# A transformer block on one core: the two row halves of the PE array get job lists of their own, with 14, 11 or 12 matmul steps a cycle

## The chip, the cores and the metric

The kernel runs on one core of a Trainium2 chip. The metric is the time of one execution on the device in microseconds (us); the median of three runs before the change is 1439.39 us. The engines are named as in the profile: PE (matmul), PEld (its weight loads), DVE (VectorE), ACT (ScalarE), POOL (GpSimd) and SP, which issues most of the transfers (DMAs).

## The reference

One pre-norm transformer block over 2048 tokens of width 512, in float32: 32 query heads of size 16 share one key head and one value head, and a gated feed-forward part of width 1792 follows.

```python
h  = x + attention(layernorm(x))       # q = x @ wq (32 heads of 16), k = x @ wk, v = x @ wv (one head)
                                       # softmax(q k^T / 4) v, heads joined, @ wo
h2 = h + (gelu(n @ w_gate) * (n @ w_up)) @ w_down      # n = layernorm(h), gelu by the tanh formula
```

## The kernel before

**Two programs woven into one.** The tokens are cut into four blocks of 512. The attention of block b runs side by side with the dense part (output projection, second norm, feed-forward) of block b-1; the dense part of the last block runs alone at the end (the tail). PE, SP and DVE work in the order in which the program writes their instructions; all three take them strictly in turn in the part that matters here.

**Attention.** A head group is four heads. For each of its 16 key chunks there are two score steps. A score step (`scores`, L358 and L362) is two matmuls on the two row halves of the array and one exp on ACT over 128x1024 elements; it needs one of two PSUM buffers `s`, so that a third step waits until the first one's exp is done. Later `weigh` (L366) multiplies the exps of a key chunk with the values, into the bank `acc`. So a head group has 32 score steps and 16 weighings.

**Cycles.** `SIZES = (6, 5, 5, 6, 5, 5)` cuts the 32 score steps of a head group into six cycles, which this document numbers 0 to 5. In a cycle the score steps come one after the other, and behind each stand some steps of dense work; all weighings that are ready stand at the cycle's end (2, 3, 2, 3, 3 and 3 key chunks in cycles 0 to 5). With cycle 5 the head group is complete, and `evacuate` sends it on: DVE copies `acc` to `oT` (L379), SP stores it to `acc_d` (L380), waits until that has landed, and issues four loads of it in another layout, `oc` (L390). At the fifth score step of a head group SP issues two loads of the queries of the next one (`load_q`, L343).

**Dense work.** Each product is split in two halves of 64 rows of the contraction, and the array's two row halves work at the same time. A step is one matmul of 64 rows on each half. `duo` (L507 to L529) computes two products at once, in two turns of 12 steps: in the first turn the lower rows work on the first product and the upper rows on the second, in the second turn the other way round. A one-column copy on DVE, `mark` (L527), stands between the turns, since both halves of a product add into the same PSUM bank. Three banks are there for products. Every cycle holds one turn, so 12 steps:

```python
LONG = {5: (0, 5, 4, 3, 0), 6: (0, 5, 3, 3, 1, 0)}    # dense steps behind each score step
```

**Feed-forward.** Per block there are 14 pieces f of the width 1792. `up(f)` computes gate and up products for a piece; the gate's tanh goes to ACT at the end of a later cycle (`gates`), and DVE forms the result, split in a high and a low part. `down` multiplies the results of four pieces (`RUNS`) with `w_down`, as four products of 12 terms for the four 128-token parts. The weights lie in DRAM, already split in high and low parts. `load_w1` (L499) loads both weights of a piece at once, 1 MB, into one of two buffers, two pieces ahead, as soon as the piece that used the buffer is done. `load_w2` (L504) loads 1 MB of `w_down` for two pieces, two loads at a time, into three buffers.

**Order of cycles.** The dense part of a block takes 47 cycles (`kinds`): four of 12 steps for the output projection, one gap, 40 of 12 steps, and two short ones. For the first block it begins with cycle 3 of a head group (`LEAD`), for the second and third with cycle 2.

Of the kernel before, what the change touches and what calls it, by code (L numbers as in the profile page):

```python
# [19 lines left out]
P = 128  # L20
# [4 lines left out]
BOUND_MAX = 30.0  # L25
BOUND_PAD = 1.02
PB = 5

FIRST_Q = 1

# [12 lines left out]
def kernel(  # L43
# [56 lines left out]
    q_d = dram.tile([H, KR, S], F32R, name="q_d")  # L100
    acc_d = dram.tile([P, 4, T], F32, name="acc_d")

    w1_d = dram.tile([FC, P, 2, 2, DC, P], F32R, name="w1_d")
    w2_d = dram.tile([FC, P, 2, D], F32R, name="w2_d")

    def split(eng_hi, hi, lo, src, eng_lo=None):
# [38 lines left out]
    def run(outer, first):  # L145
# [231 lines left out]
        def evacuate(b, g, acc):  # L377
# [17 lines left out]
                nc.vector.reciprocal(oc[:, 1, sl], oc[:, 1, sl])  # L395

            def divide():
                if c == 0:
                    o_blk[b] = [
                        sb.tile([P, DC, T], F32R, tag=f"o_{w}", bufs=1, name=f"o_{w}_{b}")  # L400
                        for w in ("hi", "lo")
                    ]
                hi, lo = o_blk[b]
                nc.vector.tensor_tensor(oc[:, 0, :], oc[:, 0, :], oc[:, 1, :], op=ALU.mult)
                split(nc.vector, hi[:, c, :], lo[:, c, :], oc[:, 0, :])


            def piece(t):
# [12 lines left out]
            if b == NB - 1 and g == NG - 1:  # L421
                last_out.append(piece)
            elif k == 1:

                outs.extend([[] for _ in range(4 if b == 0 else 1)])
                outs.extend([partial(invert, t), partial(invert, t + 1)] for t in (0, 2))
                outs.append([divide])
            if b == 0 and g == NG - 1:
                while outs:
                    take_out()  # L430
# [4 lines left out]
        def part_weights(pw):  # L435
# [24 lines left out]

            def store_1(f, k, both):
                nc.gpsimd.dma_start(
                    w1_d[f, :, :, k].bitcast(F32),
                    both.rearrange("p i (c n) -> p i c n", c=DC).bitcast(F32),
                )

# [27 lines left out]
                yield 1  # L494
            left()

        def load_w1(b, f):
            w = db.tile([P, 2, 2, DC, P], F32R, tag="w1", bufs=2, name=f"w1_{b}_{f}")
            nc.sync.dma_start(w.bitcast(F32), w1_d[f].bitcast(F32))  # L499
            return w[:, 0], w[:, 1]  # L500

        def load_w2(b, j):
# [6 lines left out]
        def duo(names, terms):  # L509

            banks = [psum1(n) for n in names]
            n = len(terms[0])
            for turn in range(2):
                for i in range(n):
                    for a in range(2):
                        k = (turn + a) % 2
                        lhsT, rhs = terms[k][i]
                        rows = slice(64 * a, 64 * a + 64)
                        nc.tensor.matmul(  # L519
                            banks[k], lhsT[rows], rhs[rows], start=(turn == 0 and i == 0),  # L520
                            stop=(turn == 1 and i == n - 1), skip_group_check=True,
                        )
                    yield 1
                if turn == 0:

                    mark = sb.tile([P, 1], F32, tag="mark", bufs=2, name=f"mark_{names[1]}")
# [19 lines left out]
        def dense(b, tail=False):  # L546
# [14 lines left out]
            w1 = {0: load_w1(b, 0), 1: load_w1(b, 1)}  # L561
            if b == 0:
                yield 0
            w2 = {}
# [129 lines left out]

            yield from start_tail() if tail else start()

            def up(f, gh, gl):
                hi, lo = w1.pop(f)
                terms = [
                    [  # L700
                        (wt[:, k, c, :], xt[:, c, :])
                        for c, (wt, xt) in (
                            [(c, (w, xT_hi)) for c in range(DC) for w in (hi, lo)]
                            + [(c, (hi, xT_lo)) for c in range(DC)]
                            if tail
                            else [
                                (c, z)
                                for c in range(DC)
                                for z in ((hi, xT_hi), (hi, xT_lo), (lo, xT_hi))
                            ]  # L710
                        )
                    ]
                    for k in range(2)
                ]
                pg, pu = yield from product([f"pg_{b}_{f}", f"pu_{b}_{f}"], terms)
                g = db.tile([P, T], F32, tag="g", bufs=2, name=f"g_{b}_{f}")
                nc.vector.tensor_copy(g, pg)  # L717
                a = db.tile([P, T], F32, tag="ga", bufs=2, name=f"ga_{b}_{f}")
                nc.vector.tensor_tensor(a, g, g, op=ALU.mult)
                nc.vector.scalar_tensor_tensor(  # L720
                    a, a, 1.0 / GELU_A, g, op0=ALU.add, op1=ALU.mult
                )

                def gate():
                    nc.scalar.activation(a, a, AF.Tanh, scale=GELU_A * GELU_C)  # L725
                    nc.vector.scalar_tensor_tensor(a, a, 1.0, g, op0=ALU.add, op1=ALU.mult)  # L726
                    nc.vector.tensor_tensor(a, a, pu, op=ALU.mult)
                    split(nc.vector, gh[:, f % 2, :], gl[:, f % 2, :], a)

                gates.append(gate)
                if tail:
                    open_gates()
                yield CUT

            def down(fs, gs, last):
                tw = [w2.pop(f // 2) for f in fs[::2]]
                for t0 in range(0, TB, 2):
                    terms = []  # L740
                    for t in (t0, t0 + 1):
                        sl = slice(t * P, (t + 1) * P)
                        terms.append([
                            (gt[:, k, sl], wt[:, k, :])
                            for (gh, gl), (hi, lo) in zip(gs, tw)
                            for k in range(2)
                            for gt, wt in ((gh, hi), (gh, lo), (gl, hi))
                        ])
                    pds = yield from product(
                        [f"pd_{b}_{fs[0]}_{t0}", f"pd_{b}_{fs[0]}_{t0 + 1}"], terms  # L750
                    )
                    for t, pd in zip((t0, t0 + 1), pds):
                        nc.vector.tensor_tensor(hs[t], hs[t], pd, op=ALU.add)
# [4 lines left out]
            prev = None  # L758
            for fs in RUNS:

                early_f = 2 if fs is RUNS[-1] else 1
                gs = []
                for n, f in enumerate(fs):
                    if f % 2 == 0:
                        gs.append([
                            db.tile([P, 2, T], F32R, tag=tag, bufs=3, name=f"{tag}_{b}_{f}")
                            for tag in ("gh", "gl")
                        ])
                    yield from up(f, *gs[-1])
                    if f + 2 < FC:  # L770
                        w1[f + 2] = load_w1(b, f + 2)
                    if fs is RUNS[-1] and n == 0:
                        w2[f // 2] = load_w2(b, f // 2)
                    if n + 1 == early_f and prev is not None:
                        yield from down(*prev, False)
                    if fs is not RUNS[-1] and n + 1 == early_f:
                        for g in fs[::2]:
                            w2[g // 2] = load_w2(b, g // 2)
                prev = (fs, gs)
            yield from down(*prev, True)  # L780

        PER = NG * KC
        work = None
# [9 lines left out]
                    evacuate(pb, pg, pacc)  # L793

        gates, behind = [], []

        def open_gates():
            while gates:
# [93 lines left out]
        for c in range(LEAD[0], (NB - 1) * NG * len(SIZES)):  # L892
# [9 lines left out]
                kind = todo.pop(0)  # L902
            if kind == "long":
                shares = LONG[size]
            elif kind == "short":
# [4 lines left out]
            ready, gates[:] = gates[:], []  # L910
            for j, share in enumerate(shares):
                score(n)
                n += 1

                if b > 0 and cb == 1 and j == 3 and outs:
                    take_out()
# [10 lines left out]
                    elif said == CUT:  # L927
                        break

            while work is not None and kind is not None and said not in (CUT, GAP):  # L930
                said = next(work)
                assert said < 0, said
            for gate in ready:
                gate()
# [6 lines left out]
            if outs:  # L941
                take_out()
        fixed.close()
        assert not outs
        held_banks.close()
# [333 lines left out]
```

## Time and profile before

| | |
|---|---|
| median of three runs | 1439.39 us (1439.32 to 1439.87) |
| the profiled execution | 1439.57 us, its span 1437.9 us |
| busy share of the span | PE 98%, ACT 72%, PEld 52%, DVE 37%, POOL 15% |
| granted clock of the array | 0.999 on average |
| chain that ended last | PE 80%, ACT 14%, DVE 2% |
| bytes moved | 180.54 MB, mean 126 GB/s |
| loads of dense weights on SP | 84 of 1 MB |

Matmuls are pipelined and their ends are modelled, so a busy PE isn't an array at its peak: the starts of the matmuls tell more than their lengths. A line of a timeline gives the start in us, the length, the engine, the line of the kernel, the operation and its operands, how many are merged into the line, and in brackets how long the engine was idle before and what ended that. The line number L519 is that of the matmul in `duo`, L541 that in the tail.

### The profile page before, as it was taken

How to read it: one execution, taken by the hardware profiler on the slowest of the kernel's cores; microseconds unless marked ns; L12 is line 12 of the kernel's file. 1: busy time of each engine (PE TensorE's matmuls, PEld its weight loads, DVE VectorE, ACT ScalarE, POOL GpSimd, SP SyncE). 2: the span in 40 equal slices, each digit the busy share in tenths (PEclk: the TensorE clock that was granted, in tenths of full speed). 3: DMA queues.
4: the chain of work that ended last, by engine and by line, in shares of the span. 5: the costliest groups of instructions: out<-in, count | busy, mean ns of one | idle time of the engine just before them, and what ended most of it. 6: DMA issues, size and time to landing. Idle time of an engine off the chain costs nothing.

```text
span 1437.9 us, 24767 instructions
## 1 busy us (share of the span) xinstructions
PE 1407.6 (98%) x10420; PEld 751.0 (52%) x10420; DVE 537.3 (37%) x931; ACT 1040.1 (72%) x1145; POOL 222.3 (15%) x301
## 2 busy tenths in 40 slices
PE   6999999999999999999999999999999999999998
PEld 5533333225555555555555555554455555557886
DVE  7422322213251423334251423423342432426665
ACT  7699999996777777776777777777777777772000
POOL 5566677731000000000000000000000000000000
PEclk9999999999999999999999999999999999999999
DMA  4456767642223332213332332203333232333551
GB/s 156 150 188 203 216 220 230 204 166 81 108 97 113 115 113 86 86 42 118 129 115 85 115 114 86 85 27 118 131 98 114 88 112 81 129 125 111 197 195 71
DMA packets 58863, 180.54 MB, mean 126 GB/s; under 512 B 8540, under 2 KB 8540, under 8 KB 51544
## 3 DMA queue, kind: packets, MB, share of 16 engines
q1 hardware_dynamic: 48912, 144.79, 29.9%
q0 software_dynamic: 9760, 34.08, 7.3%
q8 instruction: 84, 1.38, 0.4%
q14 instruction: 35, 0.29, 0.1%
q10 hardware_dynamic: 72, 0.00, 0.0%
HBM read 131.13 MB, written 47.71 MB: 124 GB/s over the span
## 4 chain that ended last, share of the span: by engine, by line
PE 80%; ACT 14%; DVE 2%; issue 1%; POOL 0%; DMA 0%; SPq 0%; ACTq 0%; DVEq 0%; POOLq 0%
PE acc L366 31%; PE s L358 18%; ACT p L362 14%; PE pu L519 6%; PE pd L519 6%; PE pg L519 5%; PE pq L184 3%; PE pg L541 3%; PE pd L541 3%; PE pu L541 3%; PE pp L519 2%; PE pxt L594 1%; PE pk L1066 0%; DVE st L1034 0%; PE pqn L222 0%
## 5 line engine op out<-in xcount | busy, mean ns | idle before, releaser
L362 ACT ACTIVATE p<-s 128x1024 f32<-128x1024 f32 x1024 | 970.4, 1057 | 249.7 <-PE s L358 249.1
L366 PE MATMUL acc<-p,v_sb 128*32 128x512 f32 x4096 | 492.3, 598 | 0.2 <-DVE oT L379 0.2
L358 PE MATMUL s<-qg,kaug 50*128 50x512 f32 x1984 | 394.2, 435 | 10.8 <-ACT p L362 7.9
L358 PEld LDWEIGHTS s<-qg,kaug 50*128 50x128 f32 x1984 | 171.5, 184 | 294.8 <-ACT p L362 183.0
L366 PEld LDWEIGHTS acc<-p,v_sb 128*32 128x32 f32 x4096 | 109.8, 109 | 239.2 <-issue 227.0
L519 PE MATMUL pg<-x2h,w 64*128 64x512 f32 x672 | 231.8, 391 | 0.0
L519 PE MATMUL pu<-x2h,w 64*128 64x512 f32 x672 | 231.7, 391 | 0.0
L120 POOL TENSOR_SCALAR rstd<-mv 128x1 f32<-128x1 f32 x16 | 3.5, 219 | 994.5 <-DVE mv L118 994.2
L519 PE MATMUL pg<-x2l,w 64*128 64x512 f32 x336 | 131.3, 391 | 0.0
L519 PE MATMUL pu<-x2l,w 64*128 64x512 f32 x336 | 131.3, 391 | 0.0
L519 PEld LDWEIGHTS pg<-x2h,w 64*128 64x128 f32 x672 | 124.7, 186 | 11.7
L519 PEld LDWEIGHTS pu<-x2h,w 64*128 64x128 f32 x672 | 124.7, 186 | 11.7
L519 PE MATMUL pd<-w,gh 64*128 64x512 f32 x672 | 105.4, 391 | 0.0
L725 ACT ACTIVATE ga<-ga 128x512 f32<-128x512 f32 x56 | 35.8, 639 | 89.1 <-DVE ga L720 89.1
L717 DVE COPY g<-pg 128x512 f32<-128x512 f32 x56 | 38.5, 688 | 118.5 <-PE pg L519 112.9
L726 DVE SCALAR_TENSOR_TENSOR ga<-ga,g 128x512 f32<-128x512 f32 x56 | 38.8, 692 | 88.9 <-ACT ga L725 88.9
L519 PEld LDWEIGHTS pd<-w,gh 64*128 64x128 f32 x672 | 63.2, 185 | 14.9 <-issue 0.7
L519 PE MATMUL pd<-w,gl 64*128 64x512 f32 x336 | 66.4, 391 | 0.0
L519 PEld LDWEIGHTS pu<-x2l,w 64*128 64x128 f32 x336 | 62.3, 185 | 7.4
L519 PEld LDWEIGHTS pg<-x2l,w 64*128 64x128 f32 x336 | 62.3, 185 | 7.3
L527 DVE COPY mark_pu<-pu 128x1 f32<-128x1 f32 x42 | 6.6, 158 | 159.1 <-PE pu L519 159.1
L395 DVE RECIPROCAL oc<-oc 128x128 f32<-128x128 f32 x64 | 56.0, 919 | 24.9 <-DMA oc<-acc_d 23.8
(233 smaller groups left out, 1281.4 us busy)
## 6 DMA issues: line engine op xcount, KB each, us to landing
w<-w_d SPq DMA_DIRECT2D x84, 1024.0 KB
qg<-q_d SPq DMA_DIRECT2D x62, 200.0 KB
q_d<-qh SPq DMA_DIRECT2D x32, 256.0 KB
acc_d<-oT SPq DMA_DIRECT2D x32, 256.0 KB
oc<-acc_d SPq DMA_DIRECT2D x128, 64.0 KB
w_d<-w_0b POOLq DMA_DIRECT2D x14, 512.0 KB, 3.4
w_d<-w_1b POOLq DMA_DIRECT2D x14, 512.0 KB, 3.5
x<-in_A_x_dram SPq DMA_DIRECT2D x16, 256.0 KB
```

The lines of the kernel that those rows point to most:

```text
L184: nc.tensor.matmul(pq, wt[:, d, c * P : (c + 1) * P], xt[:, d, :], start=(n == 0), stop=(n == 3 * DC - 1),)
L358: nc.tensor.matmul(s[:, a, :], kaug[rows, kc * P : (kc + 1) * P], qg[rows, u, :], start=True, stop=True,)
L362: nc.scalar.activation(p[:, 2 * u : 2 * u + 2, :], s, AF.Exp, scale=SCALE)
L366: nc.tensor.matmul(acc[32 * j : 32 * j + 32, :], v_sb[:, kc, :], p[:, j, :], start=(kc == 0), stop=(kc == KC - 1), skip_group_check=True,)
L395: nc.vector.reciprocal(oc[:, 1, sl], oc[:, 1, sl])
L519: nc.tensor.matmul(banks[k], lhsT[rows], rhs[rows], start=(turn == 0 and i == 0), stop=(turn == 1 and i == n - 1), skip_group_check=True,)
L527: nc.vector.tensor_copy(mark, banks[1][:, :1])
L541: nc.tensor.matmul(bank, lhsT, rhs, start=(i == 0), stop=(i == len(ts) - 1))
L594: nc.tensor.transpose(pt[:, c, :], xns[t][:, c * P : (c + 1) * P], ident)
L717: nc.vector.tensor_copy(g, pg)
L725: nc.scalar.activation(a, a, AF.Tanh, scale=GELU_A * GELU_C)
L726: nc.vector.scalar_tensor_tensor(a, a, 1.0, g, op0=ALU.add, op1=ALU.mult)
```

## The change

The 40 cycles of `duo` turns become 36 woven cycles and four as before. All gate, up and down products of a block but those of the last two runs of `down` go into one list, `plan` (28 gate and up products, and eight down products: four behind piece 5, four behind piece 9). `weave` gives each half of the array a job of its own: either the first half of the next product of the list, or the second half of a product whose first half the other half of the array has done. The upper rows start six steps (`LAG`) after the lower ones; six steps are kept as well between the end of a product's first half and the start of its second one, and between the end of a product and the next use of its bank. One half's last matmuls no longer fall together with a cycle's end. The cycles of six score steps now hold 14 steps, the others 11, and the last one of a head group 12.

The weights of a piece are now stored and loaded as two halves, gate and up, of 512 KB each, with four buffers; a buffer's next load, four halves ahead, is issued when its product is done. The loads of `w_down` for the next run are issued when the last down product of a run is done (the first two, when piece 1 is done). The work on DVE is reordered: copies out of PSUM at once, the square and cubic of the gate (`soon`), the steps behind the tanh and those of the head group's division (`lazy`) one at a time, one at each score step; the up product is multiplied in before the tanh, and its bank is free then. A woven cycle puts all its tanhs at its own end. The tail runs as before but for the order of those DVE steps, the halved loads, and the first two `down`s one piece later.

```diff
-        w = db.tile([P, 2, 2, DC, P], F32R, tag="w1", bufs=2, ...)
-        nc.sync.dma_start(w.bitcast(F32), w1_d[f].bitcast(F32))
+        w = db.tile([P, 2, DC, P], F32R, tag="w1", bufs=W1, ...)          # W1 = 4
+        nc.sync.dma_start(w.bitcast(F32), w1_d[i].bitcast(F32))
...
+        def next_w1(i):
+            if i + W1 < 2 * FC:
+                w1[i + W1] = load_w1(b, i + W1)
+        def up_plan(f, k, then):
...
+            def done(bank):
+                (leave_up if k else leave_gate)(f, bank)
+                next_w1(2 * f + k)
+                if k:
+                    then()
...
+        def weave(plan):
...
+            def choose(a):
+                for e in live:
+                    if e["half"] != a and not e["both"] and e["at"] and step >= e["at"] + LAG:
+                        e["both"] = True
+                        return [e, 0]
+                free = opened < width or ends.get(opened - width, step) + LAG <= step
+                if opened == len(plan) or not free or a == 1 and step < LAG:
+                    return None
+                name, terms, done = plan[opened]
...
+            while opened < len(plan) or live:
+                for a in range(2):
+                    if jobs[a] is None:
+                        jobs[a] = choose(a)
+                for a in range(2):
...
+                    nc.tensor.matmul(
+                        e["bank"], lhsT[rows], rhs[rows], start=i == 0 and not e["both"],
+                        stop=last and e["both"], skip_group_check=True,
+                    )
+                step += 1
...
+                    if e["both"]:
+                        e["done"](e["bank"])
+                        ends[e["i"]] = step
+                    else:
+                        nc.vector.tensor_copy(mark, e["bank"][:, :1])
+                        e["at"] = step
+                yield 1
...
-        kinds = ["long"] * 4 + ["gap"] + ["long"] * (2 * FC + 4 * (len(RUNS) - 1)) + ["short"] * 2
+        WOVEN = {6: (0, 5, 3, 3, 3, 0), 5: (0, 5, 3, 3, 0)}
+        LAST = (0, 5, 4, 3, 0)
+        kinds = (
+            ["long"] * 4 + ["gap"] + ["woven"] * 6 * len(SIZES) + ["long"] * 4 + ["short"] * 2
+        )
...
                 score(n)
                 n += 1
+                if soon or lazy:
+                    (soon or lazy).pop(0)()
```

More of the change, by code (lines that the diff above doesn't have):

```diff
@@ L560, in dense @@
             xT_lo = db.tile([P, DC, T], F32R, tag="x2l", bufs=1, name=f"x2l_{b}")
-            w1 = {0: load_w1(b, 0), 1: load_w1(b, 1)}
+            w1 = {i: load_w1(b, i) for i in range(W1)}
             if b == 0:
@@ L695, in dense, with leave_gate @@
             yield from start_tail() if tail else start()
[L697 to L715, printed above, removed]
+            gs, g_of = {}, {}
+            def next_w1(i):
+                if i + W1 < 2 * FC:
+                    w1[i + W1] = load_w1(b, i + W1)
+            def leave_gate(f, pg):
                 g = db.tile([P, T], F32, tag="g", bufs=2, name=f"g_{b}_{f}")
@@ L732, in up @@
-                gates.append(gate)
-                if tail:
-                    open_gates()
-                yield CUT
-            def down(fs, gs, last):
+                    if f % 2 == 0:
+                        gs[f // 2] = [
+                            db.tile([P, 2, T], F32R, tag=tag, bufs=3, name=f"{tag}_{b}_{f}")
+                            for tag in ("gh", "gl")
+                        ]
+                    hi, lo = (z[:, f % 2, :] for z in gs[f // 2])
+                    lazy.append(partial(
+                        nc.vector.scalar_tensor_tensor,
+                        a, a, 1.0, g, op0=ALU.add, op1=ALU.mult,
+                    ))
@@ new lines, in down_plan, with terms, done @@
+            def down_plan(fs, t, tw, then):
+                def terms():
+                    if t == 0:
+                        assert not gates and not lazy or all(j // 2 in gs for j in fs)
+                        open_gates()
+                        while lazy:
+                            lazy.pop(0)()
+                        tw.extend(w2.pop(f // 2) for f in fs[::2])
+                    return down_terms(fs, tw, t)
+                def done(bank):
+                    add_down(t, bank)
+                    if t == TB - 1:
+                        then()
+                return f"pd_{b}_{fs[0]}_{t}", terms, done
@@ L738, in down @@
+            def down(fs, last):
                 tw = [w2.pop(f // 2) for f in fs[::2]]
                 for t0 in range(0, TB, 2):
[L740 to L748, printed above, removed]
+                    terms = [down_terms(fs, tw, t) for t in (t0, t0 + 1)]
@@ L756, in down, with fetch_w2 @@
                     yield CUT
-            prev = None
+            def fetch_w2(fs):
+                for f in fs[::2]:
+                    w2[f // 2] = load_w2(b, f // 2)
+            plan, prev = [], None
             for fs in RUNS:
-                early_f = 2 if fs is RUNS[-1] else 1
-                gs = []
                 for n, f in enumerate(fs):
[L764 to L779, printed above, removed]
@@ L780, in dense @@
-            yield from down(*prev, True)
+                    then = []
+                    if fs is RUNS[-1]:
+                        if n == 0:
+                            then.append(fs)
+                    elif n == 1 and prev is None:
+                        then.append(fs)
+                    if tail:
+                        yield from up(f)
+                        for z in then:
+                            fetch_w2(z)
+                    else:
+                        for k in range(2):
+                            plan.append(up_plan(f, k, partial(
+                                lambda zs: [fetch_w2(z) for z in zs], then
+                            )))
@@ new lines, in dense @@
+                    if n != 1 or prev is None:
+                        continue
+                    if tail:
+                        yield from down(prev, False)
+                        if fs is not RUNS[-1]:
+                            fetch_w2(fs)
+                    elif fs is not RUNS[-1]:
+                        tw = []
+                        plan.extend(
+                            down_plan(prev, t, tw, partial(fetch_w2, fs)) for t in range(TB)
+                        )
+                prev = fs
@@ L782, in run @@
+            if not tail:
+                yield from weave(plan)
+                yield from down(RUNS[-2], False)
+            yield from down(RUNS[-1], True)
         PER = NG * KC
@@ L795, in run @@
         gates, behind = [], []
+        soon, lazy = [], []
         def open_gates():
@@ L904, in run @@
                 shares = LONG[size]
+            elif kind == "woven":
+                shares = LAST if cg == len(SIZES) - 1 else WOVEN[size]
             elif kind == "short":
@@ L909, in run @@
             due, said = 0, None
-            ready, gates[:] = gates[:], []
+            if kind != "woven":
+                while lazy:
+                    lazy.pop(0)()
             for j, share in enumerate(shares):
@@ L928, in run @@
                         break
-            while work is not None and kind is not None and said not in (CUT, GAP):
+            ends = kind not in (None, "woven") or kind == "woven" and todo[0] != "woven"
+            while ends and said not in (CUT, GAP):
                 said = next(work)
                 assert said < 0, said
-            for gate in ready:
-                gate()
+            open_gates()
             if work is not None and not todo:
@@ L940, in run @@
                 behind.pop(0)()
-            if outs:
+            if outs and kind == "woven":
+                lazy.extend(outs.pop(0))
+            elif outs:
                 take_out()
+        assert not lazy and not soon
         fixed.close()
```

109 lines of the change are left out of this document (93 added, 16 removed).

## The prediction

> **What bounds the kernel now.** I read the page first (busy shares, chain, costliest groups), then timelines of ACT, PE and SP over a few cycles, then the stretches of the transfers.
>
> ```profile
> PE 1407.6 (98%) x10420; PEld 751.0 (52%) x10420; DVE 537.3 (37%) x931; ACT 1040.1 (72%) x1145; POOL 222.3 (15%) x301
> PE 80%; ACT 14%; DVE 2%; issue 1%; POOL 0%; DMA 0%; SPq 0%; ACTq 0%; DVEq 0%; POOLq 0%
> L519 PE MATMUL pg<-x2h,w 64*128 64x512 f32 x672 | 231.8, 391 | 0.0
> L717 DVE COPY g<-pg 128x512 f32<-128x512 f32 x56 | 38.5, 688 | 118.5 <-PE pg L519 112.9
> ```
>
> PE is the bound, though its 98% says little, since ends are modelled. The third row says more: in front of the dense matmuls PE is idle for 0.0 us in sum, so nothing that DVE or a transfer does is waited for there today. ACT shows the cycles, because its run of exps restarts in each. These are cycles 0 to 5 of one head group, and the start of the next:
>
> ```profile
> 801.76 5.61 ACT L362 ACTIVATE p<-s 128x1024 f32<-128x1024 f32 x6 [1.65 <-PE s L358]
> 808.47 4.80 ACT L362 ACTIVATE p<-s 128x1024 f32<-128x1024 f32 x5 [1.10 <-PE s L358]
> 815.32 4.82 ACT L362 ACTIVATE p<-s 128x1024 f32<-128x1024 f32 x5 [1.53 <-PE s L358]
> 821.42 5.61 ACT L362 ACTIVATE p<-s 128x1024 f32<-128x1024 f32 x6 [1.28 <-PE s L358]
> 828.99 4.81 ACT L362 ACTIVATE p<-s 128x1024 f32<-128x1024 f32 x5 [1.46 <-PE s L358]
> 835.85 4.78 ACT L362 ACTIVATE p<-s 128x1024 f32<-128x1024 f32 x5 [2.05 <-PE s L358]
> 842.78 1.03 ACT L362 ACTIVATE p<-s 128x1024 f32<-128x1024 f32 x1 [1.63 <-PE s L358]
> ```
>
> Differences of the starts: 6.71, 6.85, 6.10, 7.57, 6.86 and 6.93 us, 41.0 in all. ACT is idle 1.1 to 2.1 us per cycle, waiting for PE's first scores. Inside a cycle it is less simple. The end of cycle 3 and the whole of cycle 4 on PE:
>
> ```profile
> 824.71 0.40 PE L519 MATMUL pg<-x2h,w 64*128 64x512 f32 x1
> ...
> 825.24 0.50 PE L358 MATMUL s<-qg,kaug 50*128 50x512 f32 x2
> 825.67 2.78 PE L366 MATMUL acc<-p,v_sb 128*32 128x512 f32 x24
> 828.39 0.73 PE L358 MATMUL s<-qg,kaug 50*128 50x512 f32 x4
> 828.95 0.39 PE L519 MATMUL pu<-x2h,w 64*128 64x512 f32 x1
> ...
> 829.88 0.39 PE L519 MATMUL pu<-x2l,w 64*128 64x512 f32 x1
> ...
> 830.12 0.45 PE L358 MATMUL s<-qg,kaug 50*128 50x512 f32 x2
> ...
> 832.27 0.40 PE L358 MATMUL s<-qg,kaug 50*128 50x512 f32 x2
> 832.60 2.78 PE L366 MATMUL acc<-p,v_sb 128*32 128x512 f32 x24
> ```
>
> Five steps stand between 828.95 and 829.88, four gaps of 0.23 us. In the cycle of five everything follows at this pace and nothing waits for ACT. In the cycle of six PE is ready for the last score at 824.71 + 0.23 = 824.94, and it starts at 825.24: 0.30 us lost to the exp that frees its buffer.
>
> **Part 1, the new shares.** A cycle of five with 11 steps loses one step behind its third score: 0.23 us, three times per head group (cycles 1, 2, 4). Does ACT become late there? The second exp of cycle 4 ends at about 828.99 + 1.03 + 0.94 (5.61 / 6) = 830.96. The score that needs it would start at 831.10 (the score at 830.12, then 0.29 to the next step and three steps of 0.23); 0.14 us remain. A cycle of six gets two more steps in front of its last score, which then starts at 824.94 + 0.46 = 825.40 instead of 825.24. Its weighing follows 0.33 us behind, as in the cycle of five (832.27 to 832.60), at 825.73 instead of 825.67: 0.06 us more, twice. So a head group of 73 steps gets shorter by 3 x 0.23 - 2 x 0.06 = 0.57 us. Three blocks have six such groups each: 18 x 0.57 = 10.3 us. Bounds: 12.4 if the two steps are wholly free, 6.7 if each six costs the full 0.16 of its last score. The six half-filled steps at the list's two ends are in the 73 already (36 products x 12 steps + 6 = 438 = 6 x 73).
>
> **Part 2, the halved loads and the head group's end.** I counted the list by hand. Product 3k opens at step 36k and ends at 36k+30; 3k+1 opens at 36k+6 and ends at 36k+36; 3k+2 opens at 36k+12 and ends at 36k+42. Weight half i+4 is loaded when half i's product ends. So for two products of three the load has only 12 steps, one cycle; before, it had two. One cycle is enough for a lone load, but not behind 2 MB of w_down. What SP does at a head group's end stands here (W, its first score, is 429.54):
>
> ```profile
> 429.54 0.73 PE L358 MATMUL s<-qg,kaug 50*128 50x512 f32 x4
> 429.68 0.69 DVE L379 COPY oT<-acc 128x512 f32<-128x512 f32 x1 [0.83 <-PE acc L366]
> 430.39 0.32 SPq L380 DMA_DIRECT2D acc_d<-oT  x1
> 432.45 1.72 SPq L390 DMA_DIRECT2D oc<-acc_d  x4
> 434.28 0.36 SPq L499 DMA_DIRECT2D w<-w_d  x1
> 434.68 0.76 SPq L343 DMA_DIRECT2D qg<-q_d  x2
> 435.49 0.40 SPq L504 DMA_DIRECT2D w<-w_d  x1
> 443.20:444.00 0.80, 0.80 (x12) 0.66 (x10) 0.00 (x0) 0.29 (x1) 0.00 (x0) 1.00 0.57 236
> 444.00:445.00 1.00, 1.00 (x12) 0.76 (x10) 0.00 (x0) 1.00 (x2) 0.00 (x0) 1.00 0.00 0
> ```
>
> SP is held until W + 4.74, as it waits for acc_d to land and issues oc. Three loads of 1 MB issued in one go:
>
> ```profile
> 695.79 0.35 SPq L499 DMA_DIRECT2D w<-w_d  x1
> 696.18 0.94 SPq L504 DMA_DIRECT2D w<-w_d  x2
> 702.00:704.50 2.50, 2.37 (x24) 0.86 (x26) 0.16 (x1) 2.48 (x4) 0.00 (x0) 1.00 1.02 419
> 704.50:705.50 1.00, 1.00 (x14) 0.17 (x4) 0.95 (x2) 0.00 (x0) 0.00 (x0) 1.00 0.50 201
> 705.50:707.50 2.00, 2.00 (x18) 1.52 (x20) 1.54 (x3) 1.57 (x2) 0.00 (x0) 1.00 0.00 0
> ```
>
> They end near 705.1 (half of the stretch at a share of 0.50), 9.3 us behind the first issue, one behind the other at 419 GB/s, 2.5 us for 1 MB (1.05 million bytes). So 2.5 MB take 9.3 - 1.27 = 8.0 us. In the second and third block the woven list begins at cycle 1 of a head group, so cycle 0 holds steps 59 to 72, 205 to 218 and 351 to 364. All three pairs of w_down loads (ends of piece 1 at step 66, of the fourth down product at 210, of the eighth at 354) fall into such a cycle 0, while SP is held. Behind each stands a weight half with 12 steps of lead:
>
> - Half 16: w_down twice, then half 16, land at W + 4.74 + 8.0 = W + 12.7. It opens at step 228, the tenth of cycle 1: 6.77 (cycle 0) + 0.56 + 9 x 0.23 + two scores of 0.24 = W + 9.9. Wait: 2.8 us.
> - Half 24: the same queue, W + 12.7. Step 372 is the eighth of cycle 1: 6.77 + 0.56 + 7 x 0.23 + 0.24 = W + 9.2. Wait: 3.5 us.
> - Half 8: in front of it half 7, w_down twice and the two query loads. In the rows above 1 MB, the query loads (0.4 MB) and 1 MB end near 443.9, 9.6 us behind 434.28, where 2 MB alone would take 9.3 - 2.5 = 6.8; so the query loads cost up to 2.8, and by their bytes alone 1.0. Half 8 lands at W + 12.7 + 2.8 + 1.3 = 16.8 (at the least 15.0). Step 84 is the first of cycle 2: 6.77 + 6.62 + 0.56 = W + 13.9. Wait: 2.9 us (1.1).
>
> PE takes its matmuls in turn, so behind the waiting one everything stands: the other half's steps, the scores, the weighing; ACT runs dry after two exps. No later slack gives it back, as PE is the bound of every cycle. That is 9.2 us per block, 18.4 in two blocks. In the first block the list begins at cycle 2, the three pairs fall one cycle behind the chain, and by the same sums the halves land 0 to 2 us before they are needed: 0.
>
> **Part 3, DVE.** A bank is taken again, and a second half begun, six steps after the end that it hangs on: seven starts apart and a score, 7 x 0.23 + 0.24 = 1.85 us, if no weighing lies between. The copy needs the last matmul's 0.39 and its own 0.69. So 0.7 us are left for DVE work that stands in front; one more DVE step of 0.69 fits, two don't. For gate products that is enough; an up product whose `soon` steps are still queued is late by some tenths. I take 1 us in all, from 0 to 8 (72 such edges per block, half of them without a weighing, 0.07 us each, three blocks). A gain is excluded by the 0.0 in the third row of the page.
>
> **Parts at nothing.** Earlier marks, the moved tanh (ACT's idle time above, 1.1 us or more, takes 0.6), the other storage layout (POOL stores it during the first quarter) and the tail, which is a chain of matmuls without gaps, and whose down products only change places:
>
> ```profile
> 1355.16 2.72 PE pg L541 x12
> ```
>
> Sum on the profiled execution: 1439.57 - 10.3 + 18.4 + 1.0 = 1448.7 us; the median of the runs lies 0.2 lower, so 1448.5.
>
> **Rivals.**
>
> - In time: the transfers land before they are needed (SP free earlier, or loads of w_down not in front). Then only the shares count: 1439.6 - 10.3 + 1.0 = 1430 us, faster. It decides where a load lands 3.5 us sooner than my sums. For it: a bandwidth mean of 126 GB/s is far from 419. Against it: the order of issue on SP is fixed by the program, and the rows above show one load behind the other. 0.12.
> - Half of it: each of the six waits is shorter by 1.5 us, 18.4 - 9 = 9.4, which cancels the gain: 1439.6. 0.14.
> - DVE late at the upper bound, 8 to 10 us more: 1457. For it: DVE works at 37% already and in turn. 0.08.
> - The clock falls. The rows at the end show the array without work:
>
> ```profile
> 1431.60:1436.30 4.70, 0.00 (x0) 0.00 (x0) 0.68 (x1) 0.00 (x0) 0.00 (x0) 1.00 0.35 123
> 1436.40:1437.90 1.50, 0.00 (x0) 0.00 (x0) 0.00 (x0) 0.00 (x0) 0.00 (x0) 0.50 0.02 5
> ```
>
> 4.7 us without a matmul kept the clock at 1.00, then it fell to 0.50. My longest waits are 3.5 us, one in each of two blocks. If the clock fell in them, and a cycle of 6.7 us behind each ran at half speed, that would be 13 us more: 1462. 0.04. [...]
>
> **How the numbers follow.** My forecast, late loads in two blocks, has 0.62 and spans 1442 to 1456. About 0.2% (2.9 us) is what can be told from no change: slower means over 1442.3, faster under 1436.5. Slower: 0.62 + 0.08 + 0.04, less a little at the lower edge, 0.73. Same: 0.14. Faster: 0.12 and a little, 0.13. The range from 1437 to 1458 leaves out the first rival and the last.
>
> **What would show it.** Cycles 1, 2 and 4 shorter by 0.23 us and cycles 0 and 3 longer by under 0.1, by the starts of ACT's runs; six PE idle times of 1 to 4 us in front of the first matmul of halves 8, 16 and 24 in the second and third block, released by a transfer, and none in the first; no idle time over some tenths released by DVE; the tail's chain as before. If those six idle times are missing, I am wrong and it is faster; if idle times released by DVE sum to more than 3 us, Part 3 was wrong.

## The result and the profile after

| | before | changed |
|---|---|---|
| median of the runs | 1439.63 us (4 runs) | 1471.09 us (1469.96 to 1472.92, 4 runs) |
| the profiled execution | 1439.57 us, span 1437.9 us | 1469.96 us, span 1468.3 us |

The ratio is 1.0218, with an interval of 1.02 to 1.0235: slower, as forecast, but by 31 us instead of 9, and outside the range. Three rows of the page of the changed kernel answer to those of before (the chain, the dense matmuls of the gate products and those of the up products; line numbers are higher by 4 and more: exps L366, scores L362, weighing L370, the woven matmul L854):

```profile
PE 84%; ACT 6%; DMA 5%; DVE 1%; SPq 1%; issue 1%; POOL 0%; ACTq 0%; DVEq 0%
L854 PE MATMUL pg<-x2h,w 64*128 64x512 f32 x672 | 216.6, 398 | 25.2 <-DMA w<-w_d 25.1
L854 PE MATMUL pu<-x2h,w 64*128 64x512 f32 x672 | 217.0, 398 | 0.3 <-DVE g L730 0.3
```

The second row is the news. Before, PE was never idle in front of the dense matmuls; now it is for 25.2 us, nearly all of it released by a load of weights. A transfer stands in the chain with 5% where it had 0%. The timeline of PE shows seven such places. The number in brackets is the idle time before the row, and what ended it:

```profile
567.59 0.47 PE L854 MATMUL pg<-x2h,w 64*128 64x512 f32 x1 [0.95 <-DMA w<-w_d]
736.67 0.47 PE L854 MATMUL pg<-x2h,w 64*128 64x512 f32 x1 [4.66 <-DMA w<-w_d]
819.15 0.76 PE L854 MATMUL pg<-x2h,w 64*128 64x512 f32 x1 [3.76 <-DMA w<-w_d]
905.21 0.76 PE L854 MATMUL pg<-x2h,w 64*128 64x512 f32 x1 [4.03 <-DMA w<-w_d]
1082.31 0.76 PE L854 MATMUL pg<-x2h,w 64*128 64x512 f32 x1 [3.92 <-DMA w<-w_d]
1164.40 0.76 PE L854 MATMUL pg<-x2h,w 64*128 64x512 f32 x1 [3.59 <-DMA w<-w_d]
1251.99 0.47 PE L854 MATMUL pg<-x2h,w 64*128 64x512 f32 x1 [4.16 <-DMA w<-w_d]
```

The last six are the first matmuls of halves 8, 16 and 24 in the second and third block, 24.1 us in sum; the 0.95 us is half 24 of the first block. A head group without such a wait shows the cycles, again by the starts of ACT's runs (the first two rows are one cycle, in which ACT ran dry for a moment):

```profile
765.36 4.69 ACT L366 ACTIVATE p<-s 128x1024 f32<-128x1024 f32 x5 [2.16 <-PE s L362]
770.41 1.06 ACT L366 ACTIVATE p<-s 128x1024 f32<-128x1024 f32 x1
772.14 4.69 ACT L366 ACTIVATE p<-s 128x1024 f32<-128x1024 f32 x5 [0.67 <-PE s L362]
778.78 4.69 ACT L366 ACTIVATE p<-s 128x1024 f32<-128x1024 f32 x5 [1.44 <-PE s L362]
784.62 5.61 ACT L366 ACTIVATE p<-s 128x1024 f32<-128x1024 f32 x6 [1.15 <-PE s L362]
792.25 4.69 ACT L366 ACTIVATE p<-s 128x1024 f32<-128x1024 f32 x5 [2.02 <-PE s L362]
798.90 4.80 ACT L366 ACTIVATE p<-s 128x1024 f32<-128x1024 f32 x5 [1.97 <-PE s L362]
805.87 1.94 ACT L366 ACTIVATE p<-s 128x1024 f32<-128x1024 f32 x2 [2.17 <-PE s L362]
```

6.78, 6.64, 5.84, 7.63, 6.65 and 6.97 us, 40.51 in all; before it was 41.0. So the new shares do what they should. But the cycles with a wait took 12.31, 12.15, 13.70, 11.35, 13.43 and 12.61 us instead of 5.84 (cycle 2, half 8) or 6.64 (cycle 1): 37.3 us more, 13.2 more than PE was idle. Where these went, the timeline of PE shows, right behind the row at 736.67 (the matmul of the other half of the array, which starts with each of these, is left out):

```profile
736.99 0.51 PE L854 MATMUL pg<-x2l,w 64*128 64x512 f32 x1
...
737.30 0.62 PE L854 MATMUL pg<-x2h,w 64*128 64x512 f32 x1
...
737.73 0.62 PE L854 MATMUL pg<-x2h,w 64*128 64x512 f32 x1
```

The steps follow each other at 0.31 and then 0.43 us instead of 0.23. The stretches around the second and the fifth wait name the reason (PEclk, behind the five engines, is the granted clock):

```profile
815.62:819.03 3.41, 0.00 (x0) 0.00 (x0) 0.00 (x0) 0.80 (x1) 0.00 (x0) 1.00 1.02 389
819.03:822.44 3.41, 3.29 (x15) 1.29 (x19) 0.00 (x0) 1.54 (x2) 0.00 (x0) 0.50 0.62 179
...
1160.37:1163.77 3.40, 0.44 (x4) 0.01 (x2) 0.16 (x1) 1.47 (x2) 0.00 (x0) 1.00 1.02 416
1163.77:1167.18 3.41, 2.78 (x14) 1.28 (x18) 0.00 (x0) 1.04 (x2) 0.00 (x0) 0.50 0.72 231
1167.19:1170.59 3.40, 3.40 (x20) 0.59 (x12) 1.12 (x2) 0.49 (x1) 0.00 (x0) 0.50 0.05 18
1170.61:1174.00 3.39, 3.39 (x30) 2.40 (x28) 1.34 (x3) 2.50 (x3) 0.00 (x0) 1.00 0.02 5
```

Behind each of the six waits the clock is 0.50, for 3.41 us (four times) or 6.83 us (twice). These are eight pieces of 3.41 us, so 13.2 / 8 = 1.65 us each. The account of the profiled execution: -9.5 for the shares (18 groups at 0.53, by the medians of the cycles), +24.1 for the waits, +13.2 at half clock, +1.2 for half 24 of the first block, which leaves 1.4 of the 30.4 for all else.

### The profile page after: what moved, and what is told of

It is laid out like the page before. It is cut to its first block, busy times and chain, and to the rows that moved or that the text cites. A ratio compares the mean times of both kernels' runs of the same rounds, so it can differ in the third digit from the quotient of the medians.

```text
span 1468.3 us, 25088 instructions
## 1 busy us (share of the span) xinstructions
PE 1418.2 (97%) x10420; PEld 761.2 (52%) x10420; DVE 544.7 (37%) x985; ACT 1036.0 (71%) x1145; POOL 217.8 (15%) x301
## 4 chain that ended last, share of the span: by engine, by line
PE 84%; ACT 6%; DMA 5%; DVE 1%; SPq 1%; issue 1%; POOL 0%; ACTq 0%; DVEq 0%
PE acc L370 30%; PE s L362 18%; PE pu L854 8%; PE pg L854 7%; ACT p L366 6%; PE pd L854 5%; DMA w<-w_d 4%; PE pq L188 4%; PE pg L553 3%; PE pd L553 3%; PE pu L553 3%; PE pd L531 2%; PE pp L531 2%; DMA acc_d<-oT 1%; PE pk L1231 1%
## 5 line engine op out<-in xcount | busy, mean ns | idle before, releaser
L366 ACT ACTIVATE p<-s 128x1024 f32<-128x1024 f32 x1024 | 967.0, 1059 | 284.6 <-PE s L362 284.4
L370 PE MATMUL acc<-p,v_sb 128*32 128x512 f32 x4096 | 497.7, 603 | 0.1
L362 PE MATMUL s<-qg,kaug 50*128 50x512 f32 x1984 | 398.8, 434 | 5.4 <-ACT p L366 4.4
L362 PEld LDWEIGHTS s<-qg,kaug 50*128 50x128 f32 x1984 | 174.8, 185 | 286.0 <-ACT p L366 161.2
L854 PE MATMUL pg<-x2h,w 64*128 64x512 f32 x672 | 216.6, 398 | 25.2 <-DMA w<-w_d 25.1
L370 PEld LDWEIGHTS acc<-p,v_sb 128*32 128x32 f32 x4096 | 110.6, 110 | 243.5 <-issue 231.4
L854 PE MATMUL pu<-x2h,w 64*128 64x512 f32 x672 | 217.0, 398 | 0.3 <-DVE g L730 0.3
L854 PEld LDWEIGHTS pg<-x2h,w 64*128 64x128 f32 x672 | 118.2, 189 | 40.6 <-issue 26.5
L854 PE MATMUL pg<-x2l,w 64*128 64x512 f32 x336 | 124.5, 399 | 0.0
L854 PEld LDWEIGHTS pu<-x2h,w 64*128 64x128 f32 x672 | 117.7, 188 | 12.1 <-DVE g L730 0.7
L854 PE MATMUL pu<-x2l,w 64*128 64x512 f32 x336 | 124.0, 396 | 0.0
L854 PE MATMUL pd<-w,gh 64*128 64x512 f32 x384 | 81.5, 391 | 0.0
L1075 DVE SCALAR_TENSOR_TENSOR ga<-ga,g 128x512 f32<-128x512 f32 x72 | 49.8, 691 | 69.6 <-ACT ga L733 68.3
L800 DVE TENSOR_TENSOR h<-h,pd 128x512 f32<-128x512 f32 x48 | 31.8, 684 | 115.7 <-PE pd L854 65.7
L383 DVE COPY oT<-acc 128x512 f32<-128x512 f32 x32 | 22.1, 692 | 141.0 <-PE acc L370 140.9
L854 PEld LDWEIGHTS pu<-x2l,w 64*128 64x128 f32 x336 | 58.9, 188 | 6.1
L854 PEld LDWEIGHTS pg<-x2l,w 64*128 64x128 f32 x336 | 59.1, 189 | 5.4
L730 DVE TENSOR_TENSOR g<-g,pu 128x512 f32<-128x512 f32 x56 | 38.3, 683 | 40.4 <-PE pu L854 30.4
```

What stands on the lines that cost most here:

```text
L362: nc.tensor.matmul(s[:, a, :], kaug[rows, kc * P : (kc + 1) * P], qg[rows, u, :], start=True, stop=True,)
L366: nc.scalar.activation(p[:, 2 * u : 2 * u + 2, :], s, AF.Exp, scale=SCALE)
L370: nc.tensor.matmul(acc[32 * j : 32 * j + 32, :], v_sb[:, kc, :], p[:, j, :], start=(kc == 0), stop=(kc == KC - 1), skip_group_check=True,)
L730: nc.vector.tensor_tensor(g, g, pu, op=ALU.mult)
L854: nc.tensor.matmul(e["bank"], lhsT[rows], rhs[rows], start=i == 0 and not e["both"], stop=last and e["both"], skip_group_check=True,)
L1075: (soon or lazy).pop(0)()
```

## Experiments

The first four ran beside runs of the kernel before with a median of 1439.08 us (9 runs), the next two beside 1439.13 us, the last beside 1439.33 us (7 runs each). Theory W is the prediction's mechanism (weight halves queued behind w_down at a head group's end), with the clock as what the waits bring with them.

**The loads of w_down two product ends later.**

```diff
-            lambda zs: [fetch_w2(z) for z in zs], then
+            lambda zs: [fetch_later(z) for z in zs], then
...
+            def ended(last):
+                for z in list(put_off):
+                    if z[0] == 0 or last:
+                        put_off.remove(z)
+                        w2[z[1]] = load_w2(b, z[1])
+                    z[0] -= 1
```

`ended` is called at the end of every product; the loads behind a run's last down product are put off in the same way.

> The changed kernel, with each pair of w_down loads issued two product ends later, behind the two weight halves with 12 steps of lead. Theory W (the time went to six waits on a weight half that stands behind 2 MB of w_down, 24 us, and to the array's half clock behind each, 13 us; the shares themselves gain 9.5 us): 1432 us, from 1430 to 1435, no PE idle time over 1 us in the woven cycles, clock 1.00 throughout. Rival Q (four half buffers with 12 steps of lead are too few whatever stands in front): the waits stay, 1460 us or more.

Measured: 1431.47 us, ratio 0.9946 (0.9932 to 0.9959), faster than both kernels. Its row of the gate products, and all the woven time in one stretch:

```profile
L854 PE MATMUL pg<-x2h,w 64*128 64x512 f32 x672 | 211.8, 392 | 0.0
365.00:1290.00 925.00, 921.22 (x7564) 500.47 (x7563) 335.27 (x613) 702.55 (x764) 6.98 (x16) 1.00 0.30 103
```

The idle time is 0.0 again, the clock 1.00 throughout. Rival Q is out: the lead of 12 steps is enough when w_down isn't in front. So the order of issue of the w_down pairs, three in each block, is the whole loss, and the shares are a gain: the waits and all that hangs on them cost 1471.1 - 1431.5 = 39.6 us. The gain over the kernel before is 7.6 us, not the shares' whole 9.5; where the rest goes was not taken apart.

**Only the second load of each pair put off.** The first stays where it was:

```diff
-                put_off.extend([n, f // 2] for n, f in zip((2, 2), fs[::2]))
+                put_off.extend([n, f // 2] for n, f in zip((0, 2), fs[::2]))
```

> The changed kernel, with only the second w_down load of each pair two product ends later, so that 1 MB less stands in front of the late weight half. Theory W: each of the six waits shorter by 2.5 us, from about 4.0 to about 1.5 us, and too short for the clock to fall: 1432 + 9 = 1441 us. Rival R (the clock falls at any such wait, however short): 11 us more, 1452 us. Rival Q: 1460 us or more.

Measured: 1445.9 us (1443.54 to 1447.55), ratio 1.004 (1.0025 to 1.0056): between the two. The waits shrank as W has it, by 2.4 us each on average, to 9.7 in sum. But W had them too short for the clock to fall, and at two of them it fell all the same, at the first and the last of these rows:

```profile
733.76 0.46 PE L854 MATMUL pg<-x2h,w 64*128 64x512 f32 x1 [2.63 <-DMA w<-w_d]
895.72 0.47 PE L854 MATMUL pg<-x2h,w 64*128 64x512 f32 x1 [1.87 <-DMA w<-w_d]
1228.08 0.47 PE L854 MATMUL pg<-x2h,w 64*128 64x512 f32 x1 [1.71 <-DMA w<-w_d]
```

The 1.71 us made it fall, the 1.87 us did not. So it is not the length of a wait alone that decides; what does, the section on the hardware reads from all the kernels.

**The even shares of before, with the late loads.**

```diff
-        WOVEN = {6: (0, 5, 3, 3, 3, 0), 5: (0, 5, 3, 3, 0)}
+        WOVEN = {6: (0, 5, 3, 3, 1, 0), 5: (0, 5, 4, 3, 0)}
```

> As late_w2, but with 12 steps in every cycle, the shares of the kernel before (0,5,4,3,0 and 0,5,3,3,1,0); the list's six extra steps stand at the end of its last cycle. Theory W (the gain comes from the shares alone): the cycles last 41.0 us per head group as before, 1432 + 9.5 + 4 = 1445 us. Rival V (the gain comes from the weave, which has no turn end at a cycle's end): about 1432 us.

Measured: 1444.37 us, ratio 1.0036 (1.0023 to 1.005). ACT's runs in it have the starts of before:

```profile
803.45 5.61 ACT L366 ACTIVATE p<-s 128x1024 f32<-128x1024 f32 x6 [2.16 <-PE s L362]
810.16 4.81 ACT L366 ACTIVATE p<-s 128x1024 f32<-128x1024 f32 x5 [1.10 <-PE s L362]
817.04 4.82 ACT L366 ACTIVATE p<-s 128x1024 f32<-128x1024 f32 x5 [1.54 <-PE s L362]
```

6.71 and 6.88 us for cycles 0 and 1, where before had 6.71 and 6.85; the medians of the other four agree with before within 0.02 us. So the gain comes from the shares alone. Weaving by itself costs 5.3 us: with 12 steps a cycle the six half-filled steps of the list no longer fit, and one cycle in each block takes them, with 8.1 to 8.3 us instead of 6.7 or 6.9 (3 x 1.4 = 4.2 us); the other 1.1 us were not located.

**Sixteen idle matmuls in front of the late halves.** Their results are overwritten; they only keep the array at work.

```diff
+                    if b > 0 and name in (f"pg_{b}_4", f"pg_{b}_8", f"pg_{b}_12"):
+                        for _ in range(16):
+                            nc.tensor.matmul(
+                                e["bank"], xT_hi[:, 0, :P], xT_hi[:, 0, :],
+                                start=True, stop=True, skip_group_check=True,
+                            )
```

> The changed kernel, with 16 full matmuls of no use (3.5 us) into the empty bank in front of the first matmul of weight halves 8, 16 and 24 in the second and third block; their results are overwritten. Theory W: the transfers are waited for as before, but the array isn't idle over 1.2 us and the clock stays at 1.00: 13 us less, 1458 us. Rival S (the slow matmuls behind the waits have another cause, such as the transfers): 1471 us, and the granted clock as before.

Measured: 1460.52 us, ratio 1.0146 (1.013 to 1.0161). The waits stand where they stood, filled with work that does nothing, and the kernel is 10.6 us faster for it. One place stayed without matmuls for 1.74 us in one piece, and there alone the clock fell:

```profile
L860 PE MATMUL pg<-x2h,w 64*128 64x512 f32 x672 | 213.1, 393 | 4.9 <-DMA w<-w_d 4.9
1156.55:1159.94 3.39, 1.65 (x10) 0.79 (x8) 0.00 (x0) 0.00 (x0) 0.00 (x0) 1.00 0.76 202
1159.95:1163.36 3.41, 3.41 (x19) 0.78 (x21) 1.12 (x2) 1.54 (x2) 0.00 (x0) 0.50 0.09 36
```

So here the half clock is a consequence of the array's idleness, and neither of the transfers nor of a load that lands: the loads are the same, PE is idle in front of these matmuls for 4.9 us instead of 25.2, and the clock falls at one of the six places instead of all.

**The second block's dense part one cycle later,** so that its list begins at cycle 2 as the first block's does:

```diff
-        LEAD = (3, 2, 2)
+        LEAD = (3, 3, 2)
```

> The changed kernel, but in the third block's dense part too (block 2, the one counted from 0 whose woven list began at cycle 1 of a head group) the list begins one cycle later, as in the first block's. So there the w_down pairs are no longer issued in the cycle in which the next head group's stored result is loaded back, and one cycle more of the next block's attention is left over at the end. Theory W (the waits come from the w_down pair queued behind the four loads of oc, in the cycle that follows a head group's end): of the six waits the three at 732, 815 and 901 us go, with the half clock behind them (12.36 us of wait and about 7 us of half clock): about 1452 us. Rival A (where the list begins does not matter; the pair in front of the weight half alone makes it late): six waits stay, 1471 us. Rival C (the loads only come late elsewhere): three waits remain in those places but shorter, as the 0.92 us of the first block: 1454 to 1458 us.

(What the expectation calls the third block is the second in the count used elsewhere here, the one with the waits at 732, 815 and 901 us.) Measured: 1451.53 us, ratio 1.0089 (1.0072 to 1.0106). Of the second block's three waits 0.81 us is left, in front of half 24. The first block has 1.06 us, the third its three (3.04, 3.73 and 4.08), 12.7 us in sum:

```profile
L854 PE MATMUL pg<-x2h,w 64*128 64x512 f32 x672 | 213.9, 395 | 12.7 <-DMA w<-w_d 12.7
895.73 0.47 PE L854 MATMUL pg<-x2h,w 64*128 64x512 f32 x1 [0.81 <-DMA w<-w_d]
1062.89 0.46 PE L854 MATMUL pg<-x2h,w 64*128 64x512 f32 x1 [3.04 <-DMA w<-w_d]
```

So a pair of w_down loads in front of a half isn't enough for a long wait; it takes what the head group's end puts on the same queue as well. One cycle of the list's place is worth 19.6 us.

**Six idle matmuls instead of sixteen.**

> The changed kernel with six full matmuls of 512 columns (about 1.3 us of work, into a bank that the product is about to clear) in front of the first step of halves 8, 16 and 24 in the last two woven blocks. The waits of 3.6 to 4.6 us shrink to idle times of 2.3 to 3.3 us, the loads land when they did. Theory F (the array's clock falls only where it is idle for a whole window of 3.4 us): no half clock, so 1471 less 13.4 us, about 1458 us. Rival G (shorter idle times do it too, as the 1.68 and 2.60 us in the kernel with only the second load of each pair put off): half the six places or more still fall to half clock, 1464 to 1471 us.

Measured: 1472.34 us (1469.94 to 1473.28), ratio 1.0226 (1.0209 to 1.0243). The waits did not shrink in three places (4.06, 4.21 and 4.62 us remain), so for theory F it tells less than was meant. The clock fell at four of the six places, as G has it. And of two places with equal idle times one fell and one didn't:

```profile
817.33:820.73 3.40, 1.75 (x14) 0.87 (x16) 0.00 (x0) 0.15 (x1) 0.00 (x0) 1.00 1.00 363
820.74:824.14 3.40, 3.40 (x20) 0.85 (x16) 1.12 (x2) 1.54 (x2) 0.00 (x0) 0.50 0.44 133
1162.07:1165.48 3.41, 1.75 (x8) 1.11 (x9) 0.02 (x1) 0.86 (x1) 0.00 (x0) 1.00 1.01 387
1165.48:1168.89 3.41, 3.41 (x32) 1.00 (x30) 1.06 (x2) 1.54 (x2) 0.00 (x0) 1.00 0.56 191
```

F, which wants 3.4 us without work, is out: 1.65 us did it. Why six matmuls let the halves land later in three places is open. For half 24 of both blocks the trace shows that the first of the load's 16 completion events came as elsewhere, 8.3 to 8.4 us behind the first issue of w_down, but the last at 10.5 and 10.9 instead of 8.6 to 8.7.

**The query loads in cycle 3 instead of cycle 0.**

```diff
-                if kc == 2 and b * NG + g + 1 < NB * NG:
+                if kc == 9 and b * NG + g + 1 < NB * NG:
```

> The changed kernel, but the two query loads of the next head group are issued at the 19th score step of a head group (cycle 3) instead of the fifth (cycle 0), so that they no longer stand among the w_down pair and the weight halves. Theory Q1 (the forecast waits of 18.4 us became 23.9 because the query loads share the 16 engines with the late halves: 0.4 MB, 1.0 us by their bytes): halves 16 and 24 land 1.0 to 1.1 us sooner in both blocks, half 8 by 1.0 to 2.8 us sooner, so the six waits sum to 14 to 18 us instead of 23.9, and with 0 to 6 us less at half clock the time is 1457 to 1465 us. Rival Q2 (the queries do not matter, something else makes the loads longer than the 2.5 MB in 8.0 us that was counted): the waits stay at 24 us and the time at 1471 us.

Measured: 1459.68 us, ratio 1.0142 (1.0125 to 1.0159). The waits sum to 17.3 us, within Q1's numbers, but not as Q1 spread them (halves 8, 16, 24 of the second block, then 8 and 16 of the third):

```profile
731.25 0.47 PE L854 MATMUL pg<-x2h,w 64*128 64x512 f32 x1 [1.19 <-DMA w<-w_d]
811.62 0.46 PE L854 MATMUL pg<-x2h,w 64*128 64x512 f32 x1 [3.28 <-DMA w<-w_d]
898.20 0.76 PE L854 MATMUL pg<-x2h,w 64*128 64x512 f32 x1 [4.41 <-DMA w<-w_d]
1071.81 0.46 PE L854 MATMUL pg<-x2h,w 64*128 64x512 f32 x1 [0.71 <-DMA w<-w_d]
1152.32 0.47 PE L854 MATMUL pg<-x2h,w 64*128 64x512 f32 x1 [3.45 <-DMA w<-w_d]
```

Half 8, in front of which the query loads were issued, waits 3.5 and 3.2 us less. For halves 16 and 24, which were issued ahead of them, nothing clear changes (-0.5, +0.4, -0.1 and, at the last place, 4.29 instead of 4.16). For these Q2 is nearer: something else makes their loads longer than was counted.

## Why the prediction was right in its direction and wrong in its size

**Part 1, the new shares: right.** Forecast 0.57 us per head group, measured 0.53, so 9.5 us instead of 10.3. Cycles 1, 2 and 4 are shorter by 0.21 to 0.24 us, cycles 0 and 3 longer by 0.06 to 0.08. The kernel with late loads and the one with even shares besides differ in the shares alone, and by 12.9 us, the six steps at the list's end among them.

**Part 2, the places: right.** All six waits stand where the hand count put them, each released by the load it named. The first block, for which none was forecast, has one of 0.95 us, which costs 1.2. That it takes the head group's end is shown by the second block's later list, that it takes w_down by the late loads.

**Part 2, the size: this term was too small, 18.4 us instead of 24.1.** SP's times were right. These are its rows in the group of half 16 (first score at 805.25):

```profile
806.10 0.32 SPq L384 DMA_DIRECT2D acc_d<-oT  x1
808.19 1.72 SPq L394 DMA_DIRECT2D oc<-acc_d  x4
809.95 0.94 SPq L516 DMA_DIRECT2D w<-w_d  x2
810.99 0.41 SPq L511 DMA_DIRECT2D w<-w_d  x1
811.45 1.06 SPq L347 DMA_DIRECT2D qg<-q_d  x2
```

w_down goes out at W + 4.70 (forecast 4.74). But PE starts on the half 9.2 us behind that and not 8.0 (halves 16 and 24 of both blocks: 8.8 to 9.2). The step that failed here is the reading of the three loads issued at 695.79. I let them end at 705.1, by the share of a stretch; the last of the third load's 16 completion events in that trace comes at 705.55, which is 9.76 us behind the first issue and not 9.3. So the same count gives 8.5 us for 2.5 MB. In the changed kernel the last completion event of halves 16 and 24 comes 8.6 to 9.1 us behind the issue of w_down, and PE starts 0.13 or 0.14 us later.

For half 8 the query loads cost 3.2 to 3.5 us, above the 2.8 that I took as their most. The 2.8 came from the same kind of reading: the 1 MB behind the query loads, issued at 435.49, has its last completion event at 444.55 and not near 443.9, which makes it 3.0. With these events the same sums give waits of 3.3, 4.0 and 3.6 us for halves 16, 24 and 8, so 21.8 us in two blocks: the reading is 3.4 of the missing 5.7 us, and the rest was not taken apart. For halves 16 and 24 the query loads are not the reason, as their waits without them show, and nor is the next half's load: without the query loads the half lands 1.29 us behind the second w_down, and the next half 1.27 us behind that, one behind the other (by the events of half 16, second block, in the kernel with late query loads).

**The rival on the clock: this step failed.** It had 0.04. I read the row of 4.7 us without matmuls at clock 1.00 as a limit: a shorter wait keeps the clock. The same stretch, cut where the windows lie, says something else:

```profile
1429.54:1432.95 3.41, 2.01 (x9) 1.31 (x8) 1.39 (x3) 0.00 (x0) 0.00 (x0) 1.00 0.51 186
1432.95:1436.36 3.41, 0.00 (x0) 0.00 (x0) 0.00 (x0) 0.00 (x0) 0.00 (x0) 1.00 0.24 84
1436.37:1437.90 1.53, 0.00 (x0) 0.00 (x0) 0.00 (x0) 0.00 (x0) 0.00 (x0) 0.50 0.02 5
```

The clock fell 3.41 us behind 1432.95, but the idle time had begun 1.4 us before that, inside a window that was still more than half full of work. So the row gives no wait that is safe. It fits a window of 3.41 us with a grid of its own. In the changed kernel each fall behind a wait comes a whole multiple of 3.41 us behind the other (819.03 to 1163.77 is 101 windows of 3.4133 us). And in the kernel before this fall comes 414 times 3.4133 us behind 23.25, where the trace's record of the clock begins; the starts of the matmuls on 512 columns, 0.41 to 0.43 us apart until then, come 0.23 or 0.24 us apart from there on. I should have taken the row as one fall behind a window that was idle from end to end, not as a wait that keeps the clock.

The rival's price was wrong as well, and only luck brings its 13 us beside the measured 13.2. It was two waits with a loss of a whole cycle of 6.7 us behind each, since I took it for my longest wait alone, 3.5 us, one in each block. Measured are six waits, with eight pieces of 3.41 us behind them that cost 1.65 us each.

**What the two steps make.** From the forecast sum of 1448.7 us to the 1470.0 of the profiled execution are 21.3 us: 13.2 for the half clock, which the sum had at nothing, 5.7 for the size of the waits, 1.2 for the first block, 0.8 for the shares, -1.0 for the DVE term and 1.4 for all else, DVE's measured 0.3 included.

**Half of it, the second rival.** The kernel with one load of each pair put off has nearly its waits, 9.7 us instead of 9.4, and comes to 1445.9 instead of 1439.6. In the profiled execution (1447.55) two falls of the clock lengthen their cycles by 1.8 and 1.9 us beyond the waits, and the tail takes 144.8 us where it has 143.4 in the changed kernel, which was not looked into.

**Part 3, the tail: right.** DVE releases 0.3 us in front of the up products, less than forecast. The tail, from the last exp to the end of the span, takes 143.4 us (before 143.8).

## What to carry to other kernels

A buffer that comes free later in the cycle shortens the lead of its next load. Ask what else the same queue issues just then, and put loads with slack (here w_down, which was needed much later) behind those without; that order alone was worth 40 us. Price an idle array twice, once as the wait (here 24.1 us) and once as the slow clock behind it (13.2 us). And read a row on the clock along its window (3.41 us in these traces), not as the length of one idle time.

## What the runs showed of the hardware

The six falls of the clock behind the waits of the changed kernel come at 737.11, 819.03, 904.36, 1081.85, 1163.77 and 1252.52, which is 24, 25, 52, 24 and 26 times 3.413 us from one to the next. I laid a grid of this step through the falls in the changed kernel and in the five experiments that show any (all but the one with both loads late and the one with the even shares), and took the idle share of each of its windows that ran at full clock in the woven part. In all 17 windows that were idle for 0.67 or more the clock fell at the window's end; the six of the changed kernel were idle for 0.84 to 1.00. In none of those with 0.43 or less did it fall. Of six windows idle for 0.48 to 0.51, three fell and three did not. So in these traces two thirds of a window always sufficed, and half of one sometimes. This is read from the traces, with the modelled ends of the matmuls; no run moved a wait along the grid on purpose, and what decides at one half is open.

A window at half clock was followed by a second one where it was itself idle for 0.16 or more (six times), and by full speed where it was idle for 0.13 or less. So a long wait that reached far enough over a window's end paid twice, as at 1163.77, where it reached 0.6 us into the next window and the clock stayed at 0.50 for 6.83 us.
